# Side work of a Fourier-mixing and attention kernel moved to other steps, and two PSUM tags exchanged

## The chip, the core and the metric

The kernel runs on one core of a Trainium2 chip. The time is device microseconds (us) of one execution; three executions of the kernel before gave 740.35, 734.36 and 738.96, so the median is 738.96 us. Each core has a matrix engine (TensorE, PE in the profile, with PEld for the loading of weights), a vector engine (VectorE, DVE), a scalar engine (ScalarE, ACT), GpSimd (POOL) and SyncE (SP), which here only issues transfers. Every engine works through its own list of instructions in the order in which the program wrote them; engines wait for each other through semaphores.

## What is computed

The output is two results side by side. The first, A, is an attention with 32 heads of 18 columns over 2048 rows in four segments, with a memory that is carried from segment to segment. The second, B, filters x in the Fourier domain:

```
X = rfft2(x)             # x: 2048 x 576
X = X * (w_r + 1j * w_i) # 2048 x 289
y = irfft2(X, s=(2048, 576))
```

The change touches B's two transforms, the splitting of A's weights, and two small mask tiles of A.

## The kernel before

The order of the whole program is written out by hand: the scheduler leaves it as it stands, so each engine's list follows the order in which the Python code emits instructions. Four stages follow each other on the matrix engine.

**Forward transform (`forward`, L108 to L196).** The 2048 rows are 16 x 128, and unit u of 16 is one block of 128 rows. In step u of a loop over 20 steps, `f1(u)` multiplies the unit by the column tables in 14 matmuls into one of three two-bank PSUM tiles (tag f1), and `c1(u-3)` multiplies an older unit by its 128-point tables in 12 matmuls into two one-bank tiles (tag c1, two buffers). Float32 accuracy is kept by splitting every operand into a high and a low part, each rounded for the matmul. So around them run, in this order in a step: ACT's `ev0(u-1)`, which copies f1's result as X0, and `evz(u-4)`, which copies c1's result out as Z and so frees its banks; the first half of `prep(u+2)` (DVE sums and differences eo, L125; ACT's rounded copy eh, L127); DVE's `ev1(u-1)` (X1, the low part, L149); a call of the pace, below; the second half of `prep` (DVE el, L131 and L132); the matmuls of f1; a load of the next input or, from step 12, a step of `first` (loads and splits of A's first x); the matmuls of c1; a load of cfw; and from step 2 one step of `load_w`, which loads one tile of A's wqk and splits the tile that was loaded two steps before (`wsplit`: ACT copy L403, DVE subtraction L405; the last of five row blocks takes two DVE instructions of 64 partitions, L405 and L406). wqk has ten tiles, five row blocks by two column halves of 576.

**The pace.** The radix-4 butterflies and twiddles between the two transforms (`bf` L206, `tws`, `stage1`, `middle`, `last`) are generators of 266 steps in all, mostly one DVE instruction each, which work on Z in SBUF. `Pace.take(f)` runs f of them at the place where it is called. `projections` shares out what the forward loop left, less ten, evenly over its units.

**Projections (`projections`, from L533).** Four groups of 13 units: nine `qk_unit` (14 matmuls of 512 columns, then DVE and ACT work that splits the result in three, of which L478 is the DVE subtraction, L482 and L485 ACT copies and L484 a matmul that the next unit waits behind) and four `v_unit` (ACT copies L509 into tile vt, two buffers, which is stored to vD). In the last group a hook opens the pools of the inverse transform at unit 9 and from unit 11 calls `ysplit`, which splits a finished Z block into the high and low parts Y0 (ACT, L280) and Y1 (L281). `ysplit` runs the pace on until its group of four blocks has finished.

**Inverse transform (`inverse`, L283 to L341).** In step u, `i2(u,(0,1))` and `i2(u,(2,))` multiply Y(u) by tables civ in 12 and 6 matmuls into two PSUM tiles; ACT (L326, L333) and DVE (L328, L334) copy them out as T0 and T1 and free the two banks; `i3(u-2)` multiplies T by the tables itab in 14 matmuls into two more banks; `out` combines and stores. Two tags, i2 and i3, have two buffers each: the tag that is asked for first takes banks 3 and 4, the other 5 and 6. Beside it runs `prologue`, which starts A's attention with `s1`; its mask tiles tri and idb are made by `masks` (L582), and PE's first use of them is L645.

**Attention** follows, with 133 steps from 360 us on. The change does not touch it.

Of the kernel before, what the change touches and what calls it, by code (L numbers as in the profile page):

```python
# [5 lines left out]
F32=mybir.dt.float32; F32R=mybir.dt.float32r  # L6
# [96 lines left out]
class FFT:  # L103
# [4 lines left out]
    def forward(s,xp,cp,pp,wl,xs,consts):  # L108

        nc,io=s.nc,s.io; v=nc.vector  # L110
        xin={}; cw={}; C={}; eh={}; el={}; F={}; X={}
        def load(u):
            xin[u]=xp.tile([128,2,3,128],F32,name="xin",bufs=3)
            nc.sync.dma_start(xin[u],io["xb"][u])
        def loadc(u):
            a,b=BORD[u]
            cw[u]=cp.tile([128,2,384],F32R,name="cfw",bufs=4)
            nc.gpsimd.dma_start(cw[u],io["cfw"][4*a+b].rearrange("p (h m) -> p h m",h=2))
        def prep(u,halves=False):

            x=xin.pop(u)
            eo=xp.tile([128,2,3,128],F32,name="eo",bufs=2)
            h=xp.tile([128,2,3,128],F32R,name="eh",bufs=3)
            for r,op in enumerate((OP.add,OP.subtract)):
                v.tensor_tensor(eo[:,r],x[:,0],x[:,1],op=op)  # L125
                if halves: nc.scalar.copy(h[:,r],eo[:,r])
            if not halves: nc.scalar.copy(h,eo)  # L127
            yield
            l=xp.tile([128,2,2,128],F32R,name="el",bufs=3)
            for w in (slice(0,1),slice(1,2)) if halves else (slice(0,2),):  # L130
                v.tensor_tensor(l[:,w],eo[:,w,:2],h[:,w,:2].bitcast(F32),op=OP.subtract)  # L131
                v.tensor_tensor(h[64:97,w,2],eo[64:97,w,2],h[64:97,w,2].bitcast(F32),op=OP.subtract)  # L132
            eh[u],el[u]=h,l
            yield
        def f1(u):
            p=pp.tile([128,2,512],F32,name="f1",tag="f1")
            h,l=eh.pop(u),el.pop(u)
            for r in range(2):
                L=[(h[:,r,0],tab[:,0,r,0]),(h[:,r,1],tab[:,0,r,1]),(h[:,r,0],tab[:,1,r,0]),(h[:,r,1],tab[:,1,r,1]),
                   (l[:,r,0],tab[:,0,r,0]),(l[:,r,1],tab[:,0,r,1]),(h[:99,r,2],tab2[:99,r])]  # L140
                for n,(x,t) in enumerate(L):
                    nc.tensor.matmul(p[:,r,:FP],x,t,start=n==0,stop=n==6)  # L142
            F[u]=p
        def ev0(u):
            x=xp.tile([128,2,FP],F32R,name="X0",bufs=3); X[u]=[x]
            nc.scalar.copy(x,F[u][:,:,:FP])
        def ev1(u):
            x=xp.tile([128,2,FP],F32R,name="X1",bufs=3)
            v.tensor_tensor(x,F.pop(u)[:,:,:FP],X[u][0].bitcast(F32),op=OP.subtract)  # L149
            X[u].append(x)  # L150
        def evz(u):
            a,b=BORD[u]
            for r,p in enumerate(C.pop(u)): nc.scalar.copy(s.Z[:,b,a,r],p[:,:FP])
        def c1(u):
            a,b=BORD[u]; x=X.pop(u); cc=cw.pop(u)
            for r in range(2):
                p=pp.tile([128,512],F32,name="c1",tag="c1")
                n=0
                for (i,hl) in ((0,0),(0,1),(1,0)):
                    for q in range(2):  # L160
                        k=(0 if q==0 else 2) if r==0 else (1 if q==0 else 0)
                        nc.tensor.matmul(p[:,:FP],cc[:,hl,k*128:(k+1)*128],x[i][:,q],start=n==0,stop=n==5)
                        n+=1
                C.setdefault(u,[]).append(p)
        load(0)
        tab=cp.tile([128,2,2,2,FP],F32R,name="ftab",bufs=1)
        tab2=cp.tile([128,2,FP],F32R,name="ftab2",bufs=1)
        nc.gpsimd.dma_start(tab[:,0],io["ftab"][:,:4*FP].rearrange("p (r c f) -> p r c f",r=2,c=2))
        late=consts()
        nc.gpsimd.dma_start(tab[:,1],io["ftab"][:,4*FP:].rearrange("p (r c f) -> p r c f",r=2,c=2))  # L170
        nc.gpsimd.dma_start(tab2,io["ftab2"].rearrange("p (r f) -> p r f",r=2))
        load(1); load(2); late()
        for u in range(2): loadc(u)
        p=[prep(u,True) for u in range(2)]
        for i in range(2):
            for x in p: next(x)
        load(3)
        s.pace=Pace(61+165+40)
        for u in range(20):
            p=prep(u+2) if u+2<16 else iter(())  # L180
            if 0<u<17: ev0(u-1)
            if 3<u: evz(u-4)
            if u%4==3 and u>6: s.pace.add(s.stage1((u-7)//4))
            next(p,None)
            if 0<u<17: ev1(u-1)
            if u<14: s.pace.take(1)
            next(p,None)
            if u<16: f1(u)
            if u+4<16: load(u+4)
            elif u<18: next(xs,None)  # L190
            if 2<u<19: c1(u-3)
            if 0<u<15: loadc(u+1)
            if 1<u: next(wl,None)
            if u>13: s.pace.take(2)
        for _ in wl: pass
        for _ in xs: pass  # L196
    def bf(s,x,y,inv):
# [85 lines left out]
    def inverse(s,yl,pp):  # L283

        nc,io=s.nc,s.io; tab,tab2=s.itab,s.itab2; v=nc.vector
        T={}; po={}; Yt=s.Yt
        def i2(u,cs):
            Y=Yt[u]; cc=s.civ[u]
            p=pp.tile([128,len(cs),256],F32,name="i2",tag="i3" if u==1 else "i2")
            for k,c in enumerate(cs):  # L290
                n=0
                for (i,hl) in ((0,0),(0,1),(1,0)):
                    for q in range(2):
                        o=128 if q==0 else 0
                        m=128 if c<2 else 99
                        nc.tensor.matmul(p[:m,k],Y[i][:,q,c*128:c*128+m],cc[:,hl,o:o+256],start=n==0,stop=n==5)  # L296
                        n+=1
            return p
# [21 lines left out]
        for u in range(18):  # L320
            if u>15: flush()
            if u<16:
                h=yl.tile([128,3,256],F32R,name="T0",bufs=3); l=yl.tile([128,2,256],F32R,name="T1",bufs=3)
                T[u]=(h,l)
                p=i2(u,(0,1))
                nc.scalar.copy(h[:,:2],p)  # L326
                if u+2<16: s.ysplit(u+2)
                v.tensor_tensor(l,p,h[:,:2].bitcast(F32),op=OP.subtract)  # L328
                yield
                flush()  # L330
                p=i2(u,(2,))
                Yt.pop(u); s.civ.pop(u)
                nc.scalar.copy(h[:99,2],p[:99,0])  # L333
                v.tensor_tensor(h[64:97,2],p[64:97,0],h[64:97,2].bitcast(F32),op=OP.subtract)  # L334
                if u+4<16: s.load_civ(u+4)
                yield
            if u>1:
                yield from i3(u-2)
                out(u-2)
                s.pace.take(1)  # L340
# [44 lines left out]
class ATT:  # L385
# [21 lines left out]
    def load_w(s,nm,n,wp,st,w,tag,bufs):  # L407
        nc,io=s.nc,s.io
        s.wh[nm]=wp.tile([128,5,n],F32R,name=nm+"h"); s.wl[nm]=wp.tile([128,5,n],F32R,name=nm+"l")
        J=[(t,o) for t in range(5) for o in range(0,n,w)]; q=[]  # L410
        for i in range(len(J)+bufs-1):
            if i<len(J):
                t,o=J[i]
                x=st.tile([128,512 if tag=="xl" else w],F32,name="raw",tag=tag,bufs=bufs)[:,:w]
                nc.sync.dma_start(x,io[nm][:,t*n+o:t*n+o+w])
                q.append((t,o,x))
            if i>=bufs-1:
                t,o,x=q.pop(0)
                s.wsplit(nm,x,t,o,w)
            yield  # L420
# [451 lines left out]
    def prologue(s):  # L872

        nc,io=s.nc,s.io
        yield
        s.load_v(0)
        q=s.stack_dmas(1,0)+s.stack_dmas(1,1)+s.stack_dmas(2,0)+s.stack_dmas(2,1)+[lambda: s.load_v(1)]+s.stack_dmas(3,1)
        for i in range(2): yield
        s.masks()
        i=0  # L880
        for t in range(10):
            for _ in s.s1(t):
                for _ in range(1+(i%24==0)):
                    if q: q.pop(0)()
                i+=1
                yield
            if 2<=t<6: nc.gpsimd.dma_start(s.Ks[t-2][108:110].rearrange("p h c -> p (h c)"),io["neg1"])
            if t in (3,7): m=s.mpath(t//4); next(m)
            if t in (4,8): next(m); next(m,None)
        assert not q  # L890
# [147 lines left out]
def emit(nc,tc,io):  # L1038
    def pool(es,name,bufs=1,**kw):
        return es.enter_context(tc.tile_pool(name=name,bufs=bufs,reuse_waits="tile",**kw))  # L1040
    with ExitStack() as L0:
# [8 lines left out]
        F=FFT(nc,tc,io,zp); F.tp=A.ftp=ftp  # L1050
        with tc.manual_schedule():
# [5 lines left out]
            with ExitStack() as es:  # L1057
# [3 lines left out]
                def hook(g,i):  # L1061
                    if g==3 and i==9:
# [2 lines left out]
                        F.yp=pool(Ri,"yp",2); F.Yt={}; ci=pool(Ri,"ci")  # L1065
                        tc.swap_default_side()
                        F.inv_setup(ci)
                    if g==3 and i>10: F.ysplit(i-11,nc.vector)
                    if g==3 and i==0: q0.extend(A.stacks0(x0))
                    if g==3 and i>0: q0.pop(0)()  # L1070
                q0=[]
# [38 lines left out]
```

## Time and profile before

The profiled execution took 736.84 us; its instructions span 735.1 us, so 1.7 us lie around them. It lies 2.1 us below the median of the three executions.

| stage | on PE, us from the start |
|---|---|
| forward transform | 9.2 to 76.0 |
| projections | 76.0 to 284.3 |
| inverse transform, with the attention's prologue | 284.5 to about 360 |
| attention, output projections | to the end at 735.1 |

Over the span PE is busy for 691.1 us, DVE for 553.4, ACT for 457.9, POOL for 204.2. A row of the timeline gives the start in us, the duration in us of the merged group, engine, line, operation, out<-in with shapes, the count, and in brackets the idle time before it with what ended it. Matmuls overlap: the start of the next row, not the end of a row, tells when PE was free. Times of "waits" are us in total, number of times, and the longest.

### The profile page before, as it was taken

Reading aid. Unit: us, or ns where it says so; the run is one execution under the profiler, and the core shown is the slowest. Engines: PE = TensorE matmul, PEld = TensorE weight load, DVE = VectorE, ACT = ScalarE, POOL = GpSimd, SP = SyncE. Lnnn points to the kernel's source line nnn. Section 1 sums busy time; section 2 is a strip of 40 time slices with the busy share of each in tenths; the row PEclk is TensorE's granted clock in tenths of the full one; section 3 lists DMA queues with packets and bytes.
Section 4 is the critical chain, followed back from the end, with each engine's and each line's share of the span. In section 5 each row is a group of like instructions: output and inputs, shape, how many; then the busy total and the mean of one; then the engine's idle time right before and its main releaser. Section 6 shows DMA issues by size and latency. Waiting matters only on the chain.

```text
span 735.1 us, 14249 instructions
## 1 busy us (share of the span) xinstructions
PE 691.1 (94%) x4879; PEld 496.6 (68%) x4879; DVE 553.4 (75%) x1285; ACT 457.9 (62%) x1012; POOL 204.2 (28%) x405
## 2 busy tenths in 40 slices
PE   4998999999999999999999999999999899998897
PEld 4988779879779788899744444443665345653396
DVE  6999879899799788787688878876567575668333
ACT  3666796585585664444487777776566566568521
POOL 2111000100200112565065335462334832325100
PEclk9999999999999999999999999999999899999999
DMA  9884435655373468899547656777456565431231
GB/s 337 264 267 148 144 116 180 197 173 160 133 236 113 169 206 277 213 219 219 179 99 185 168 149 162 179 177 145 117 142 161 142 156 131 108 115 41 70 123 64
DMA packets 83243, 121.04 MB, mean 165 GB/s; under 512 B 11352, under 2 KB 50630, under 8 KB 83036
## 3 DMA queue, kind: packets, MB, share of 16 engines
q1 hardware_dynamic: 76580, 104.11, 49.9%
q0 software_dynamic: 6592, 16.03, 8.0%
q8 instruction: 38, 0.62, 0.3%
q14 instruction: 33, 0.27, 0.1%
HBM read 81.78 MB, written 38.24 MB: 163 GB/s over the span
## 4 chain that ended last, share of the span: by engine, by line
PE 70%; DMA 13%; DVE 7%; ACT 5%; issue 3%; POOL 1%; SPq 1%; ACTq 0%; DVEq 0%; POOLq 0%
PE pj L459 14%; PE pv L709 8%; PE po L829 7%; PE pjv L459 7%; PE s L636 4%; PE i L307 4%; PE i L296 3%; PE s L644 3%; PE s L679 3%; DMA x<-qkD 2%; DMA Ks<-qkD 2%; DMA Qs<-qkD 2%; PE pn L778 2%; PE po L858 2%; PE s L683 2%
## 5 line engine op out<-in xcount | busy, mean ns | idle before, releaser
L640 DVE CUSTOM_DVE_ANT_0 junk<-s,mask 128x512 bf16<-128x512 f32 (+1 forms) x256 | 141.2, 551 | 62.6 <-PE s L636 59.0
L646 DVE TENSOR_REDUCE mx<-s 128x4 f32<-128x512 f32 x128 | 87.9, 687 | 12.0 <-PE s L645 9.2
L692 POOL TENSOR_SCALAR_AFFINE_SELECT P<-P 128x512 f32<-128x512 f32 x116 | 70.0, 634 | 73.9 <-ACT P L680 66.0
L709 PE MATMUL pv<-P,vs 128*32 128x512 f32 (+3 forms) x1024 | 89.3, 445 | 0.3 <-DVE P L694 0.3
L680 ACT ACTIVATE P<-s 128x512 f32<-128x512 f32 x128 | 76.3, 596 | 17.4 <-PE s L679 15.0
L689 ACT ACTIVATE P<-s 128x256 f32<-128x256 f32 x128 | 49.1, 384 | 50.9 <-PE s L688 50.9
L685 ACT ACTIVATE P<-s 128x512 f32<-128x512 f32 x128 | 76.0, 594 | 0.3 <-PE s L684 0.3
L459 PE MATMUL pj<-x,wqkh 128*128 128x512 f32 x162 | 56.5, 409 | 0.0
L206 DVE TENSOR_TENSOR Z<-t,t 128x290 f32<-128x290 f32 (+1 forms) x96 | 48.4, 553 | 0.1
L206 DVE TENSOR_TENSOR t<-Z 128x580 f32<-128x580 f32 x64 | 46.0, 754 | 0.0
L506 POOL MEMSET vt<- 128x32 f32 x16 | 2.3, 161 | 153.8 <-PE pm L516 128.7
L636 PE MATMUL s<-Ks,Qs 108*128 108x512 bf16 (+1 forms) x128 | 42.2, 330 | 0.1
L142 PE MATMUL f<-ftab,eh 128*128 128x290 f32 (+1 forms) x160 | 31.4, 315 | 10.1 <-DMA ftab<-ftab 10.1
L296 PE MATMUL i<-civ,Y 128*128 128x256 f32 (+1 forms) x288 | 38.5, 285 | 1.5 <-POOL Y L281 0.9
L296 PEld LDWEIGHTS i<-civ,Y 128*128 128x128 f32 (+1 forms) x288 | 35.9, 181 | 2.3 <-POOL Y L281 1.3
L709 PEld LDWEIGHTS pv<-P,vs 128*32 128x32 f32 x1024 | 22.4, 109 | 21.9 <-issue 14.6
L645 PE MATMUL s<-tri,idb 128*128 128x256 bf16 x128 | 35.2, 275 | 1.3 <-ACT idb L585 1.3
L307 PE MATMUL i<-itab,T 128*128 128x290 f32 (+1 forms) x224 | 36.0, 309 | 0.0
L459 PE MATMUL pj<-xh,wqkl 128*128 128x512 f32 x90 | 35.5, 395 | 0.0
L459 PE MATMUL pj<-x,wqkl 128*128 128x512 f32 x90 | 35.5, 395 | 0.0
L459 PE MATMUL pj<-xh,wqkh 128*128 128x512 f32 x90 | 35.5, 395 | 0.0
L459 PEld LDWEIGHTS pj<-x,wqkh 128*128 128x128 f32 x162 | 30.4, 188 | 7.2 <-issue 0.6
(211 smaller groups left out, 1830.5 us busy)
## 6 DMA issues: line engine op xcount, KB each, us to landing
qkD<-sp SPq DMA_DIRECT2D x36, 384.0 KB
Ks<-qkD SPq DMA_DIRECT2D x72, 144.0 KB
x<-qkD SPq DMA_DIRECT2D x60, 144.0 KB
Qs<-qkD SPq DMA_DIRECT2D x60, 144.0 KB
xin<-xb SPq DMA_DIRECT2D x16, 384.0 KB
cfw<-cfw POOLq DMA_DIRECT2D x16, 384.0 KB, 4.9
civ<-civ POOLq DMA_DIRECT2D x16, 384.0 KB, 7.6
vs<-vD SPq DMA_DIRECT2D x16, 330.0 KB
```

What stands on the lines that cost most here:

```text
L206: v.tensor_tensor(o,a,b,op=op)
L296: nc.tensor.matmul(p[:m,k],Y[i][:,q,c*128:c*128+m],cc[:,hl,o:o+256],start=n==0,stop=n==5)
L307: nc.tensor.matmul(p,x,t,start=n==0,stop=n==6)
L459: s.nc.tensor.matmul(out,a,b,start=i==0,stop=i==len(L)-1)
L636: nc.tensor.matmul(out,Q[:108,h,128*i:128*i+128],K[:108,h,:128*(i+1)],start=True,stop=True)
L640: nc.vector.tensor_tensor_reduce(out=junk[:,:w],in0=src,in1=s.mask[:,512-w:],scale=1.0,scalar=-3.0e38, op0=OP.add,op1=OP.max,accum_out=s.m ...
L646: nc.vector.tensor_reduce(out=s.mx[k][:,hh],in_=pa.rearrange("p (b c) -> p b c",c=128),axis=mybir.AxisListType.X,op=OP.max)
L680: nc.scalar.activation(P[0][:,hh],p0,AF.Exp,scale=SC)
L685: nc.scalar.activation(P[1][:,hh],p1,AF.Exp,scale=SC)
L692: if k<29: nc.gpsimd.affine_select(out=x,in_=x,pattern=pat+[[1,128]],compare_op=OP.is_ge,fill=0.0,base=0,channel_multiplier=-1)
L709: nc.tensor.matmul(s.pvt[32*hh:32*hh+32,128*j:],vt[:,j,19*h:19*h+32],mv[0][:,hh,mv[1]],start=j==0,stop=j==2,skip_group_check=True)
L829: nc.tensor.matmul(ps,a[t][:r,c],b[:r,t,w],start=i==0,stop=i==14)
```

## The change

It does five things, and no instruction's shape changes.

1. In `forward`, steps 9 to 13 no longer call `load_w`; those calls come in steps 14 to 18. So tiles 5 to 9 of wqk are split five steps later, and tiles 7 to 9 are also loaded later: on SP's queue they now stand behind the last inputs and between the loads of A's first x. `load_w` goes over the column halves in its outer loop, so that the five tiles split early are the first half of the columns.
2. The pace's step at step 7 goes, and from step 14 it takes one step in place of two, then three in steps 18 and 19: 16 steps in the loop in place of 19.
3. `c1(14)` writes into an f1 tile in place of two c1 tiles.
4. In `inverse`, the tag i3 is used for the matmuls of u=0 in place of u=1. So u=0 takes banks 3 and 4 and u=1 banks 5 and 6 as before, but from then on `i2` uses banks 5 and 6, and `i3` banks 3 and 4.
5. Y(0), Y(1) and Y(2) are split in the last three units of the projections with DVE subtractions (before: Y(0) and Y(1), one unit later); Y(3) is split at the end of step 0 of the inverse with POOL subtractions, Y(4) in step 2. `masks` is emitted at the start of `prologue`'s work, one of its steps ahead of the first `s1`.

In each engine's list this comes to the following. PE: the same list, but for the 12 matmuls of `c1(14)` and the banks. ACT: the copies of the splits stand elsewhere; Y(0)'s copies now stand ahead of L482 of the last `qk_unit`, tri and idb behind the copies of u=2 and not behind those of u=3. POOL: two subtractions fewer. DVE: two subtractions more, and 32 steps of the pace in place of 27 between the last L478 of the projections and the first L328 of the inverse.

```diff
         def c1(u):
             a,b=BORD[u]; x=X.pop(u); cc=cw.pop(u)
+            if u==14: P=pp.tile([128,2,512],F32,name="f1",tag="f1")
             for r in range(2):
-                p=pp.tile([128,512],F32,name="c1",tag="c1")
+                p=pp.tile([128,512],F32,name="c1",tag="c1") if u!=14 else P[:,r]
...
-            if u<14: s.pace.take(1)
+            if 7<u<14: s.pace.take(1)
...
-            if 1<u: next(wl,None)
-            if u>13: s.pace.take(2)
+            if 1<u<9 or u>13: next(wl,None)
+            if u>13: s.pace.take(1 if u<18 else 3)
...
-            p=pp.tile([128,len(cs),256],F32,name="i2",tag="i3" if u==1 else "i2")
+            p=pp.tile([128,len(cs),256],F32,name="i2",tag="i3" if u==0 else "i2")
...
-                if u+2<16: s.ysplit(u+2)
+                if 1<u<14: s.ysplit(u+2)
...
                 v.tensor_tensor(h[64:97,2],p[64:97,0],h[64:97,2].bitcast(F32),op=OP.subtract)
+                if u==0: s.ysplit(3)
                 if u+4<16: s.load_civ(u+4)
...
-        J=[(t,o) for t in range(5) for o in range(0,n,w)]; q=[]
+        J=[(t,o) for o in range(0,n,w) for t in range(5)]; q=[]
...
         yield
+        s.masks()
         s.load_v(0)
...
         for i in range(2): yield
-        s.masks()
...
-                    if g==3 and i>10: F.ysplit(i-11,nc.vector)
+                    if g==3 and i>9: F.ysplit(i-10,nc.vector)
```

## The prediction

> **What bounds the kernel now.** I read the whole span first, then busy time by stage, then who waited for whom on PE, then the timelines of the two stages that the change touches.
>
> ```profile
> span 735.1 us, 14249 instructions
> 36.00:61.00 25.00, 23.28 (x163) 21.92 (x162) 24.60 (x43) 15.31 (x30) 3.17 (x6) 1.00 0.80 243
> 160.00:180.00 20.00, 20.00 (x148) 18.95 (x147) 19.60 (x36) 12.17 (x25) 0.17 (x2) 1.00 0.58 182
> 180.00:280.00 100.00, 99.46 (x556) 84.02 (x556) 84.10 (x158) 65.68 (x127) 10.88 (x40) 1.00 0.52 174
> 302.00:360.00 58.00, 57.90 (x452) 54.72 (x451) 44.97 (x110) 25.42 (x62) 27.01 (x39) 1.00 0.85 208
> PE c L162 <- ACT Z L153: 4.4, 8, 1.2
> PE s L645 <- ACT idb L585: 1.3, 1, 1.3
> ```
>
> The columns of a stretch are its length, then busy us of PE, PEld, DVE, ACT, POOL, then clock, DMA share, GB/s. In the projections (160 to 280) and the inverse (302 to 360) PE is the bound, at 99% and more, so time taken from other engines there is worth nothing. In 36 to 61, the second half of the forward transform, DVE is full (24.60 of 25) and PE is not. Of PE's waits, 4.4 us are c1's for the copies of Z, all in the forward transform, and 1.3 us are for idb at the start of the inverse. These stages can give something, and only these.
>
> ```profile
> 32.83 0.70 PE L142 MATMUL f<-ftab,eh 128*128 128x290 f32 x4
> 36.35 0.70 PE L142 MATMUL f<-ftab,eh 128*128 128x290 f32 x4
> ...
> 56.56 0.70 PE L142 MATMUL f<-ftab,eh 128*128 128x290 f32 x4
> 60.67 0.69 PE L142 MATMUL f<-ftab,eh 128*128 128x290 f32 x4
> 65.66 0.70 PE L142 MATMUL f<-ftab,eh 128*128 128x290 f32 x4
> 70.11 3.48 PE L162 MATMUL c<-X,cfw 128*128 128x290 f32 x24 [0.77 <-ACT Z L153]
> 74.32 1.88 PE L162 MATMUL c<-X,cfw 128*128 128x290 f32 x12 [0.73 <-ACT Z L153]
> 76.04 0.63 PE L459 MATMUL pj<-x,wqkh 128*128 128x512 f32 x2
> 31.10 1.02 DVE L125 TENSOR_TENSOR eo<-xin 128x384 f32<-128x384 f32 x2
> 34.93 1.02 DVE L125 TENSOR_TENSOR eo<-xin 128x384 f32<-128x384 f32 x2
> 43.17 1.02 DVE L125 TENSOR_TENSOR eo<-xin 128x384 f32<-128x384 f32 x2
> 46.62 0.76 DVE L405 TENSOR_TENSOR wqkl<-raw,wqkh 128x576 fp32r<-128x576 f32 x1
> 47.30 1.02 DVE L125 TENSOR_TENSOR eo<-xin 128x384 f32<-128x384 f32 x2
> 58.99 0.75 DVE L405 TENSOR_TENSOR wqkl<-raw,wqkh 64x576 fp32r<-64x576 f32 x1
> 45.02 0.67 ACT L403 CAST wqkh<-raw 128x576 fp32r<-128x576 f32 x1
> 46.13 0.70 ACT L153 COPY Z<-c 128x290 f32<-128x290 f32 x2
> ```
>
> The rows of L142 are f1(7), (8), (13), (14), (15). A step is 3.52 us while PE sets it (32.83 to 36.35), and 4.11 us in steps 9 to 13 (56.56 to 60.67). One DVE step is 4.13 us (43.17 to 47.30), of which the split of a weight tile is 0.68 (46.62 to 47.30), or 1.5 where it is two instructions of 64 partitions (0.75 each, 58.99). Without the split it would be 3.45, just under PE's 3.52.
>
> **The change, part by part.** (1) Forward, steps 9 to 13. The split goes: DVE 4.13 to 3.45, ACT's copy goes as well, and PE's 3.52 takes over. But step 8 now holds both a butterfly step and the two-instruction split. DVE's L125 of steps 6 and 7 lies 3.83 apart (31.10, 34.93); with no butterfly in step 7, step 8 starts at 34.93 + 3.83 = 38.76 and lasts 4.13 + 0.82 = 4.95, so the L125 of step 9 comes at 43.71. From such a row to the end of the Z copy that frees c1's bank are 3.3 us before (43.17, to 46.13 plus half of 0.70), 0.6 of it the weight copy of 45.02, which is gone in step 9. Hence c1 of step 10 starts at 43.71 + 2.7 + 0.1 = 46.5. With every step at 3.52, f1(10) would start at 36.35 + 7.04 = 43.4 and its c1 1.8 later (3.52 less 1.74, half of the 24 matmuls of 70.11), at 45.2: PE comes 1.3 late, once, and DVE then keeps ahead. f1(14) starts at 36.35 + 6 x 3.52 + 1.3 = 58.8 in place of 60.67.
>
> (2) Forward, steps 14 to 18. The step from f1(14) to f1(15) took 4.99, as its DVE work held a 1.5 split; now 3.52, so f1(15) starts at 62.3, 3.4 early. The 0.77 wait of c1(13) stays: its bank comes free only behind the X0 copy that waits for c1(12). c1(15) now needs the copy of unit 13, not 14, which stood behind A's x splits: its 0.73 goes. The projections start at 76.04 - 3.4 - 0.73 = 71.9: **4.1 us earlier**. The moved splits (0.67 ACT, 0.68 to 1.5 DVE each) lie beside the matmuls: after step 13 DVE has no more prep, and X1, a split of x, a split of wqk and a butterfly, each like the rows of 0.7 to 0.8, make some 3 us a step. The first unit needs only the first column half, split by step 8; the second is needed by unit 4, 14 us later. The loads of tiles 7 to 9 follow A's x on SP's queue and have two steps to land; the x loads behind them are used at 71.9 + 2 us or later. If that cover fails the price is the lateness of one load, 0 to 2 us; the trace shows no such wait, and I take 0. The bank for c1(14) held f1(13), read out long before: 0.
>
> (3) Three butterfly steps pass from the loop to the projections, about 2 us on a DVE that is idle for 15.9 us in 180 to 280: 0.
>
> (4) The inverse's start.
>
> ```profile
> 284.53 4.53 PE L296 MATMUL i<-civ,Y 128*128 128x256 f32 x36 [0.22 <-ACT vt L509]
> ...
> 293.10 2.04 PE L307 MATMUL i<-itab,T 128*128 128x290 f32 x14
> 294.97 2.30 PE L296 MATMUL i<-civ,Y 128*128 128x256 f32 x18
> 297.11 0.39 PE L644 MATMUL s<-x 108*128 108x384 bf16 x2
> 272.14 2.91 DVE L206 TENSOR_TENSOR Z<-t,t 128x580 f32<-128x580 f32 x6
> 274.97 2.77 DVE L206 TENSOR_TENSOR t<-Z 128x580 f32<-128x580 f32 x4
> 277.67 1.08 DVE L281 TENSOR_TENSOR Y<-Z,Y 128x512 fp32r<-128x512 f32 x2
> ...
> 285.19 2.54 DVE L206 TENSOR_TENSOR Z<-t,t 128x580 f32<-128x580 f32 x5
> 288.61 0.69 DVE L328 TENSOR_TENSOR T<-i,T 128x512 fp32r<-128x512 f32 x1 [0.88 <-ACT T L326]
> 289.78 0.43 DVE L334 TENSOR_TENSOR T<-i,T 33x256 fp32r<-33x256 f32 x1 [0.49 <-ACT T L333]
> 271.59 0.59 ACT L482 CAST sp<-pj 128x512 bf16<-128x512 f32 x1
> 289.56 1.83 POOL L281 TENSOR_TENSOR Y<-Z,Y 128x512 fp32r<-128x512 f32 x2 [1.83 <-ACT Y L280]
> ```
>
> PE does i2(0) and i2(1) in one run, 36 matmuls. i2(2) is 18 matmuls, 2.14 us where nothing holds it (294.97 to 297.11), but PE reached i3(0) only at 293.10, as Y(2) was still being split. Now Y(2) is ready before. What is late next is DVE. Its list from 272.14 runs without a gap to 287.7 (285.19 plus 2.54) and then starts L328. The list now holds five more butterfly steps and Y(2)'s subtractions: four of t, 2.70 (274.97 to 277.67), one of Z, 0.37 (2.91 less 2.54), and the 1.08 of 277.67, together 4.15 us. It ends at 291.9, and L328(0), L334(0), L328(1) follow in 0.69 + 0.43 + 0.69, less overlaps of 0.1, to 293.6. This matters because of the exchanged tags: i2(2) now goes into the bank that i2(1) filled, and must wait for L328(1), where before it went into i2(0)'s. So i2(2) starts at 293.6 and i3(0) at 293.6 + 2.14 = 295.7, not 293.10: **2.6 us lost**. Five butterfly steps fewer in the inverse save nothing, as PE is full there.
>
> (5) Masks. tri and idb are copied behind u=2, before PE comes to L645: the 1.30 us goes. Their two copies then delay only E(0), for which nothing waits.
>
> (6) ACT's copies of Y(0) now stand before L482 of the last qk unit and wait for DVE's first Z of 272.14: L482 moves from 271.59 to some 2.5 us later, and all of PE's v matmuls stand behind the L484 that needs it. PE reached L484 about then, so this costs from 0 to the 0.7 of one copy; I take 0.2, an estimate. The copies of vt behind L482 come later too, and with them one store; the copies that wait for its slot come long before DVE's 293.6, which covers this.
>
> (7) POOL: its two subtractions of Y(2) go; the load of civ for u=4 now stands behind Y(3)'s, about as before behind Y(2)'s. 0.
>
> Sum: -4.1 + 2.6 - 1.3 + 0.2 = **-2.6 us**. Against the profiled execution (span 735.1, time 736.84) that is a span of 732.5 and a time of 734.2; the median of the executions lies 2.1 above it, so I forecast 736.4.
>
> **A rule weighed.** Y(3)'s subtractions on POOL (1.83 us for the pair) now fall beside DVE's last butterfly steps.
>
> ```profile
> 192.70 0.82 DVE L206 TENSOR_TENSOR t<-Z 128x580 f32<-128x580 f32 x1
> 192.86 0.72 POOL L532 TENSOR_TENSOR zst<-mm,zst 126x7 f32<-126x7 f32 x1
> ```
>
> Where the two engines met, DVE's instruction took 0.82 (0.76 without), and POOL's 0.72. By the rows POOL gives way, which costs the sum 0.1. [...]
>
> **The rivals.**
> - POOL holds DVE up in the last steps: both subtractions, 1.83 us, go into DVE's list and so into i2(2)'s start: -2.6 + 1.8 = -0.8, 738.2. For it: POOL's start falls among four back-to-back steps. Against: the pair of rows above.
> - DVE's list is not the wait: i2(2) runs at once behind the 36 matmuls, at 288.9, and i3(0) at 291.0, a gain of 2.1 in place of the loss of 2.6: -7.3, 731.7. For it: Y(2) is ready, and 4.7 us of PE time hang on this. Against: DVE's list, which has no gap from 272.14 on.
> - The forward step does not fall, because the ring of X0, Z and c1 and not DVE's load sets it: only 0.73 and the 1.5 of step 14 are gained: -2.2 + 1.5 = -0.7, 738.3. Against: step 7 ran at 3.52 with the split and without the butterfly.
> - Slower: ACT's L482 behind Y(0). If DVE reaches the butterflies of 272.14 late by x, L482, L484 and all of PE behind it are late by x. It decides from x = 2.6. At x = 4, twice the 2 us of the deferred steps, the time is 738.96 + 1.4 = 740.4. For it: DVE was at 19.60 of 20 in 160 to 180. Against: 15.9 us idle in 180 to 280.
>
> **How the numbers follow.** Forecast 0.55; POOL ahead 0.13; no DVE wait 0.14; forward unchanged 0.10; slower 0.08. The forecast's own range is 734.5 to 738, from the bounds in parts 2 and 6 and half of the once-late 1.3 us. The range for 8 in 10 reaches up to the slower rival's near side and down to the case without DVE's wait: 731.5 to 739.5. One per cent, about what a measurement of this kernel can tell from no change (its three executions span 6 us), is 7.4 us: below 731.6 lies half of the case without DVE's wait and a rest for terms that I have too small, 0.13; above 746.3 nothing that I can work out, 0.05; between, 0.82.
>
> **What would show each step.** Steps of 3.5 us from f1(10) to f1(15), one wait of about 1 us in c1 of steps 9 and 10, projections from about 72 us; no wait of c1(15). A wait of PE's L296 for DVE's L328 of about 4.5 us, the longest of that stage, with DVE busy without a gap up to it; no wait for idb. POOL's subtractions of Y(3) longer than 1.83 us. The forecast is wrong if i2(2) starts before DVE's butterflies end, or if the projections start later than 73 or lose their 99%.

## The result and the profile after

The changed kernel takes 740.41 us (median of 20 executions, 737.53 to 743.52); the kernel before, in 20 executions (the three of the first section among them), 736.8. The ratio is 1.004, with a 95% interval of 1.0026 to 1.0054: slower by 1.9 to 4.0 us. The forecast was 2.6 us faster. The profiled execution took 738.24 (span 736.5). Times here are medians of all executions of a run; a ratio is worked out from the single executions, without the few in which the chip was in a slower state (one of the twelve behind the 734.04 of the run with Y(2) and Y(3) on DVE), and so is not just the quotient of two medians.

A caution for all places below: PE's first waits, for the column tables, take between 8.7 and 10.1 us in all in eight of the runs (10.1 before, 9.8 after). So places of two runs agree only to 1 or 1.5 us; lengths and waits are better compared.

The waits on PE and the busy time by stretch, with the columns of the prediction. L-numbers after the change are one or two higher than before: L480, L484, L486 are the subtraction, the second copy and the last matmul of a qk unit; L297 is i2, L329 and L335 the subtractions on T.

```profile
PE i L297 <- DVE T L329: 5.1, 1, 5.1
PE pj L486 <- ACT sp L484: 4.1, 5, 1.8
PE c L163 <- ACT Z L153: 1.4, 2, 0.8
PE i L297 <- ACT vt L511: 1.3, 1, 1.3
PE pm L518 <- ACT pk L497: 0.6, 1, 0.6
36.00:61.00 25.00, 24.25 (x174) 23.32 (x174) 24.25 (x43) 15.38 (x32) 3.70 (x7) 1.00 0.72 220
76.00:160.00 84.00, 80.28 (x430) 65.77 (x429) 73.69 (x141) 63.61 (x125) 2.75 (x18) 1.00 0.48 161
280.00:302.00 22.00, 15.66 (x110) 15.20 (x109) 16.97 (x29) 6.87 (x18) 6.20 (x12) 0.84 0.56 170
```

The forward transform gained what was meant: c1 waits 1.4 us in place of 4.4, and the wait for idb is gone. But two waits grew or are new: 4.1 us for the qk units' second copies, and 5.1 us for DVE at the inverse. The stretch 280 to 302 shows something that no part of the prediction had: a granted clock of 0.84. The timeline of PE, at the four places that matter:

```profile
58.80 0.70 PE L142 MATMUL f<-ftab,eh 128*128 128x290 f32 x4
62.32 0.69 PE L142 MATMUL f<-ftab,eh 128*128 128x290 f32 x4
66.76 1.87 PE L163 MATMUL c<-X,cfw 128*128 128x290 f32 x12 [0.77 <-ACT Z L153]
71.69 0.63 PE L461 MATMUL pj<-x,wqkh 128*128 128x512 f32 x2
81.73 0.38 PE L486 MATMUL pj<-sp,nid 128*128 128x512 bf16 x1 [1.71 <-ACT sp L484]
96.04 0.38 PE L486 MATMUL pj<-sp,nid 128*128 128x512 bf16 x1 [0.21 <-ACT sp L484]
105.99 0.38 PE L486 MATMUL pj<-sp,nid 128*128 128x512 bf16 x1 [1.80 <-ACT sp L484]
273.60 0.38 PE L486 MATMUL pj<-sp,nid 128*128 128x512 bf16 x1 [0.22 <-ACT sp L484]
284.52 4.51 PE L297 MATMUL i<-civ,Y 128*128 128x256 f32 x36 [1.25 <-ACT vt L511]
294.11 4.16 PE L297 MATMUL i<-civ,Y 128*128 128x256 f32 x18 [5.08 <-DVE T L329]
298.10 2.04 PE L308 MATMUL i<-itab,T 128*128 128x290 f32 x14
303.42 0.39 PE L638 MATMUL s<-x 108*128 108x512 bf16 x1
```

f1(14), f1(15) and the projections start at 58.80, 62.32 and 71.69; the forecast had 58.8, 62.3 and 71.9. Then the three waits of 81.73, 96.04 and 105.99 take back 3.7 us (before, 0.27 + 0.96). The first two of the next rows are of the kernel before, the others of the changed kernel; they show the stretch, what DVE did ahead of the first wait, and the busy times around the waits:

```profile
76.00:160.00 84.00, 82.63 (x439) 67.80 (x438) 71.90 (x137) 63.27 (x126) 3.04 (x18) 1.00 0.52 169
80.25 0.69 DVE L478 TENSOR_TENSOR pj<-pj,sp 128x512 f32<-128x512 f32 x1
...
73.96 2.78 DVE L207 TENSOR_TENSOR t<-Z 128x580 f32<-128x580 f32 x4
76.66 2.54 DVE L207 TENSOR_TENSOR Z<-t,t 128x580 f32<-128x580 f32 x5
79.86 0.69 DVE L480 TENSOR_TENSOR pj<-pj,sp 128x512 f32<-128x512 f32 x1
...
80.00:90.00 10.00, 8.29 (x37) 6.39 (x36) 9.12 (x20) 9.14 (x21) 0.00 (x0) 1.00 0.64 196
100.00:110.00 10.00, 8.20 (x46) 6.77 (x45) 5.93 (x13) 9.53 (x20) 0.00 (x0) 1.00 0.31 107
```

The projections start 4.35 us earlier, but the first subtraction of a qk unit only 0.4 (79.86 against 80.25): nine butterfly steps, 5.2 us in a row, stand in front of it. Near 106 it is ACT that is busy (9.53 of 10), not DVE (5.93). At the inverse, i2(2) starts at 294.11, and its 18 matmuls take 4.16 us, where 18 such matmuls took 2.30 before. What DVE and POOL did just ahead of it:

```profile
287.03 1.20 DVE L207 TENSOR_TENSOR Z<-t,t 128x290 f32<-128x290 f32 x3
288.14 4.14 DVE L207 TENSOR_TENSOR t<-Z 128x580 f32<-128x580 f32 x4
292.20 0.68 DVE L329 TENSOR_TENSOR T<-i,T 128x512 fp32r<-128x512 f32 x1
288.52 2.47 POOL L282 TENSOR_TENSOR Y<-Z,Y 128x512 fp32r<-128x512 f32 x2 [2.12 <-ACT Y L281]
```

Four steps of t took 4.14 us where four took 2.77 before: 1.37 more, just while POOL subtracted for Y(3), itself 2.47 in place of 1.83. And the clock, from the windows of 0.4 us around its two edges:

```profile
291.00:291.40 0.40, 0.00 (x0) 0.00 (x0) 0.40 (x1) 0.00 (x0) 0.40 (x1) 0.81 0.87 261
291.40:291.80 0.40, 0.00 (x0) 0.00 (x0) 0.40 (x2) 0.00 (x0) 0.40 (x2) 0.50 1.09 347
...
297.40:297.80 0.40, 0.40 (x4) 0.40 (x3) 0.11 (x1) 0.40 (x2) 0.00 (x0) 0.50 0.00 0
297.80:298.20 0.40, 0.40 (x4) 0.40 (x3) 0.40 (x1) 0.38 (x1) 0.00 (x0) 0.65 0.00 0
```

0.81 in a window is full clock for 0.25 of its 0.4 us and half clock behind, so the clock fell at 291.25; by 0.65 it came back at 298.08. It was halved for 6.83 us, two times the 3.41 of a run below. i2(2) lies wholly inside. From these rows i3(0) starts 5.00 us later than before (298.10 against 293.10). The masks give 1.46 of it back: the score matmul of 512 columns (L638, before L636) behind the first masked one started at 299.88 before, and starts at 303.42 here, 3.54 later. This profiled execution regains 2.1 us of that in the attention, which I didn't follow; the medians differ by 3.6.

### The profile page after: what moved, and what is told of

It is laid out like the page before. It is cut to its first block, busy times and chain, and to the rows that moved or that the text cites. A ratio compares the mean times of both kernels' runs of the same rounds, so it can differ in the third digit from the quotient of the medians.

```text
span 736.5 us, 14243 instructions
## 1 busy us (share of the span) xinstructions
PE 690.8 (94%) x4879; PEld 497.6 (68%) x4879; DVE 555.6 (75%) x1287; ACT 457.6 (62%) x1012; POOL 202.2 (27%) x403
## 4 chain that ended last, share of the span: by engine, by line
PE 51%; DVE 7%; DMA 5%; ACT 2%; issue 2%; POOL 1%; SPq 0%; DVEq 0%; ACTq 0%; POOLq 0%
PE pv L711 9%; PE po L831 7%; PE s L638 5%; PE i L297 4%; PE i L308 4%; PE pj L461 3%; PE s L646 3%; PE s L681 3%; PE pn L780 2%; PE s L685 2%; PE po L860 2%; DMA Qs<-qkD 2%; DVE t L207 2%; PE s L647 1%; DVE junk L642 1%
## 5 line engine op out<-in xcount | busy, mean ns | idle before, releaser
L694 POOL TENSOR_SCALAR_AFFINE_SELECT P<-P 128x512 f32<-128x512 f32 x116 | 70.0, 634 | 71.9 <-ACT P L682 64.1
L297 PE MATMUL i<-civ,Y 128*128 128x256 f32 (+1 forms) x288 | 39.7, 293 | 6.3 <-DVE T L329 5.1
L638 PE MATMUL s<-Ks,Qs 108*128 108x512 bf16 (+1 forms) x128 | 42.2, 330 | 0.1
L297 PEld LDWEIGHTS i<-civ,Y 128*128 128x128 f32 (+1 forms) x288 | 37.4, 189 | 6.8 <-DVE T L329 5.3
```

What stands on the lines that cost most here:

```text
L638: nc.tensor.matmul(out,Q[:108,h,128*i:128*i+128],K[:108,h,:128*(i+1)],start=True,stop=True)
L694: if k<29: nc.gpsimd.affine_select(out=x,in_=x,pattern=pat+[[1,128]],compare_op=OP.is_ge,fill=0.0,base=0,channel_multiplier=-1)
```

## The experiments

Theory A, from these rows: four things turned a gain into a loss. The first qk units come too early for DVE and ACT (2.5 us more of waits); DVE's list ahead of the inverse is longer, as predicted; POOL lengthens it by 1.4; and PE, standing still behind it, gets a half clock that costs 1.9. The rivals are with each run.

**The two halves.** First the forward hunks alone, then the inverse hunks alone, each on the kernel before.

```diff
-            if u<14: s.pace.take(1)
+            if 7<u<14: s.pace.take(1)
-            if 1<u: next(wl,None)
-            if u>13: s.pace.take(2)
+            if 1<u<9 or u>13: next(wl,None)
+            if u>13: s.pace.take(1 if u<18 else 3)
... (and c1(14), load_w)
```

> The forward part of the change alone (items 1 to 3), on the inverse of the kernel before. Theory A (DVE comes late to the first units of the projections, and this takes back more than half of the forward gain): projections start at about 71.7 as in the changed kernel, against 76.0 before; PE again waits about 1.7 us at the third matmul of the first qk unit and about 1.8 us near 106, against 1.2 us in all before; the v projections end about 1.4 us early. PE's first i2 starts between 283.1 and 284.5, as the copies of vt wait for stores; no wait of 5 us at the inverse and a full clock there. Time 0 to 1.4 us below the kernel before, 735.4 to 736.8. Theory B (the forward part gains its 4.1 us and all of the loss is in the inverse): 732.7.

Measured: ratio to before 0.9977 (0.9951 to 1.0003), or 1.7 us faster, with the waits of the first units at 3.7 us and no half clock at the inverse (1.00 in 280 to 302). The 4.1 of theory B (a ratio of 0.994) lies outside the interval, no change just inside it: less than the whole gain arrives, and how much does is not known more closely.

```diff
-            p=pp.tile([128,len(cs),256],F32,name="i2",tag="i3" if u==1 else "i2")
+            p=pp.tile([128,len(cs),256],F32,name="i2",tag="i3" if u==0 else "i2")
-                    if g==3 and i>10: F.ysplit(i-11,nc.vector)
+                    if g==3 and i>9: F.ysplit(i-10,nc.vector)
... (and the other splits, masks)
```

> The inverse part of the change alone (items 4 and 5), on the forward transform of the kernel before. Theory A (DVE's list is longer by five butterfly steps and Y(2), is lengthened once more by 1.4 us where POOL works on Y(3), and the wait of 5 us brings a half clock that costs 2 us): DVE's list ends 0.9 us later than in the changed kernel, i2(2) starts at about 295, with 0.5 of the clock for some 4 to 6 us, and takes about 4 us in place of 2.2; the masks give back 1.3 to 1.5. Sum 2.6 + 0.9 + 1.4 + 2.0 - 1.4 = +5.5; time 741 to 742.5. Theory B (the inverse part costs what the prediction said, 2.6 - 1.3 + 0.2): +1.5, 738.3.

Measured: 1.0034 (1.001 to 1.0058), 2.5 us slower. The interval, 0.7 to 4.3 us, leaves out theory A's 5.5 and takes in theory B's 1.5, so the time does not choose; the rows show the wait for DVE and the half clock of theory A, and say why it was less:

```profile
288.75 2.10 DVE L206 TENSOR_TENSOR t<-Z 128x580 f32<-128x580 f32 x3
289.42 3.12 POOL L281 TENSOR_TENSOR Y<-Z,Y 128x512 fp32r<-128x512 f32 x2 [2.12 <-ACT Y L280]
292.69 3.67 PE L296 MATMUL i<-civ,Y 128*128 128x256 f32 x18 [3.26 <-DVE T L328]
```

Here DVE's steps kept their 0.7 us each and POOL's pair took 3.12 (1.83 before): this time POOL gave way. The half clock came all the same (0.50 in 292.2 to 295.4). By their ratios the halves make +0.8 us together and the whole +2.9; with intervals of 2 us to either side for each half, that is no contradiction.

**The wait and the clock.** In the next run the pace leaves as many butterfly steps to the inverse as before the change.

```diff
+                if g==3 and i>9: w*=.78
                 advance()
                 pace.take(w*.4)
```

> The changed kernel with a lower pace in the last three v units, so that 11 butterfly steps (as before) in place of 6 are left for the inverse. Theory A: DVE's list ends near 288, PE's wait for DVE's subtraction on T(1) falls from 5.1 to 1 us or less, and with it the half clock goes: i2(2) starts near 289.7 in place of 294.1 (4.4 us) and takes 2.2 in place of 4.2 (2.0 us): 740.4 - 6.4 = 734.0. Theory B (the half clock has another cause than the wait): 740.4 - 4.4 = 736.0. Theory C (another thing is late next at this place, POOL's Y(3) or a load of civ): 737 to 738, with its name in PE's waits.

Measured: 0.9971 (0.9945 to 0.9997), 735.45. The wait fell to 1.83 us, not under 1, and the clock was halved all the same (0.50 in 291.4 to 294.2):

```profile
290.15 3.44 PE L297 MATMUL i<-civ,Y 128*128 128x256 f32 x18 [1.83 <-DVE T L329]
289.41 0.69 DVE L329 TENSOR_TENSOR T<-i,T 128x512 fp32r<-128x512 f32 x1 [0.55 <-DMA vD<-vt]
291.00:291.40 0.40, 0.40 (x5) 0.40 (x4) 0.00 (x0) 0.00 (x0) 0.00 (x0) 0.66 1.01 315
294.20:294.60 0.40, 0.40 (x4) 0.40 (x4) 0.38 (x1) 0.32 (x2) 0.40 (x1) 0.58 0.00 0
```

Late next, for 0.55 of the 1.83 us, was a store of a v tile (theory C had other names for it); that T1 of u=1 takes over the memory of that tile is inferred from this wait. The clock was halved from 291.13 to 294.54, 3.41 us (a later expectation calls a stretch of this length a window): so here it came behind 1.83 us of standing still. Whether standing still is the cause was tried by filling the changed kernel's wait with 36 repeated matmuls.

```diff
-                for (i,hl) in ((0,0),(0,1),(1,0)):
+                for (i,hl) in ((0,0),(0,1),(1,0))*(7 if u==1 and c==2 else 1):
+                    n%=6
```

> The changed kernel, in which PE does the last six matmuls of i2(1) seven times over (36 repeated matmuls, 4.3 us at full clock, same result), just where it waits for DVE. The wait for DVE's subtraction stays where it ends, 294.1. Theory A (PE's clock falls because PE stands still for 5 us): the clock stays at 1.00 and i2(2) takes 2.1 to 2.3 us in place of 4.16: 740.4 - 2.0 = 738.4, with more work on PE. Theory B (the clock falls for another reason): it falls again, no change, 740.4 or more.

Measured: 1.0004 (0.9983 to 1.0026), 737.58; by the ratios about 2.7 us less than the changed kernel, with more work on PE.

```profile
288.51 2.78 DVE L207 TENSOR_TENSOR t<-Z 128x580 f32<-128x580 f32 x4
289.33 3.67 POOL L282 TENSOR_TENSOR Y<-Z,Y 128x512 fp32r<-128x512 f32 x2 [2.11 <-ACT Y L281]
280.00:302.00 22.00, 21.29 (x170) 20.59 (x169) 17.95 (x34) 8.49 (x22) 8.91 (x14) 1.00 0.68 207
```

The clock is 1.00 in the whole stretch, where it was 0.84 in the changed kernel. Theory A holds: with the wait of 5.08 us filled, no half clock comes. Not all of the 2.7 us is the clock's, though. DVE's and POOL's lists are those of the changed kernel, but this time POOL gave way (3.67) and DVE's four steps took 2.78, so that DVE's list ended 1.0 us earlier (291.20 against 292.20). Next, the lower pace together with the banks of the kernel before, so that i2(2) waits for T(0) alone.

```diff
-            p=pp.tile([128,len(cs),256],F32,name="i2",tag="i3" if u==0 else "i2")
+            p=pp.tile([128,len(cs),256],F32,name="i2",tag="i3" if u==1 else "i2")
```

> The run with the lower pace in the last three v units, and with the banks of the kernel before: i2(1) in the i3 banks, so that i2(2) waits for the subtractions on T(0) and not on T(1). Theory A (what was late next there was the store of the last vt, which held the subtraction on T(1) to 289.41, and half a window of standing still is enough for the half clock): i2(2) starts at about 288.9, PE stands still under 1 us there, the clock stays at 1.00; 1.2 us of wait and 1.8 us of half clock go: 735.5 - 3.0 = 732.5. Theory B (the tag matters little, as i3(0) or i2(3) then waits for the same store): no gain or under 1 us, 734.5 to 735.5, with the wait at i3(0).

Measured: 0.9943 (0.9923 to 0.9964), 734.05.

```profile
284.60 6.66 PE L297 MATMUL i<-civ,Y 128*128 128x256 f32 x54 [1.06 <-ACT vt L511]
```

i2(0), i2(1) and i2(2) run as one group of 54 matmuls, and no half clock comes (1.00 in 280 to 302). With these two edits the rest of the change is a gain of 4 us.

**What held DVE?** DVE in place of POOL subtracts for Y(3) in the changed kernel.

```diff
-                if u==0: s.ysplit(3)
+                if u==0: s.ysplit(3,v)
```

> The changed kernel with the subtractions of Y(3) on DVE in place of POOL. Theory A (the butterfly steps that took 4.14 for four, and not 2.78, were held by POOL's subtractions): no such step is longer than 0.76 now, the subtraction on T(0) starts at 290.8 (1.4 earlier), and behind Y(3)'s 1.0 us that on T(1) starts at 293.0 to 293.4, as late as before within 0.4: 739.9 to 740.4. Theory B (they were long for a reason of DVE's own or of a memory): they stay long, the subtraction on T(1) starts at 294.4: 741.4.

Measured: 1.0041 (1.0023 to 1.0058), the time of the changed kernel, as theory A has it.

```profile
289.34 2.77 DVE L207 TENSOR_TENSOR t<-Z 128x580 f32<-128x580 f32 x4
```

The four steps of t took 2.77 again. So it was POOL's work that made them long. By what way POOL holds DVE, no run shows. No time is gained, as DVE now does the subtractions itself.

**The first units of the projections.** Four butterfly steps fewer at the end of the forward loop:

```diff
-            if u>13: s.pace.take(1 if u<18 else 3)
+            if u>13: s.pace.take(1)
```

> The changed kernel with one butterfly step instead of three in each of the last two steps of the forward loop; four butterfly steps (about 2.2 us of DVE) pass into the projections, so that DVE is free earlier for the subtraction of the first qk unit. Theory A (the butterflies that stand in front hold up the first units): PE's first wait for the second sp copy, 1.71 at 81.7, falls to 0.5 or less; the one near 106, where ACT's queue of twiddle copies is in front, stays within 1 us of what it was; the list of the inverse gains nothing. 740.4 - 1.3 = 739.1. Theory B (the projections simply start too early for the weights and x tiles that are split beside them): the wait stays, 740.4, or returns in the next unit.

Measured: 1.0038 (1.001 to 1.0066), 740.61. The first wait went, and 1.18, 0.62 and 1.12 came at 87, 103 and 109, 2.9 in place of 3.7, with 0.94 for a copy of pk at 119. The little that PE won became a longer wait for DVE at the inverse (6.6 us). That is what theory B has, but four steps may have been too few; the dealing below tells more. The same edit in the version with the lower pace and the banks of before:

> The three together: lower pace in the last three v units, banks of the kernel before, one butterfly step in the last two steps of the forward loop; everything else as changed. If the terms add: 732.5 - 1.3 = 731.2, about 0.8% below the kernel before and faster than both. If what the forward part wins is taken back by DVE or by the stores of v, as half of it was in the changed kernel: as the run without the last edit, 732.5.

Measured: 0.995 (0.9922 to 0.9978), 733.59: the terms don't add. The edit in the forward part, with only the masks of the inverse part:

```diff
         yield
+        s.masks()
         s.load_v(0)
...
         for i in range(2): yield
-        s.masks()
```

> The forward part with one butterfly step in the last two steps, and of the inverse part the masks alone (splits and banks as in the kernel before). The forward part alone gave 735.0; the masks take away PE's wait of 1.3 us for idb, and the last edit of the loop about 1.3: 732.4. If copying the masks earlier only moves ACT's work before the copies of T and E (rival), the wait at this place comes back under another name and the time is 733.7.

Measured: 0.9939 (0.9918 to 0.996), 732.52; the wait for idb is gone and 2.9 us remain at the first units. The diff of the masks alone, on the kernel before:

> The masks alone moved ahead, all else as in the kernel before. As the prediction's part 5 has it: PE's wait of 1.3 us for idb goes and nothing takes its place: 1.3 below the kernel before, ratio 0.998. Rival (the two copies, 0.5 us on ACT, hold up the copies of T that stand behind them): no change.

Measured: 0.9968 (0.9946 to 0.9991); the interval takes in the predicted 0.998. Now the dealing of the first nine units, on the kernel with the forward part and the masks:

```diff
-                w=tot/(36+16*2.4)*(1.0 if i<9 else 2.4)
+                w=tot/(36+16*2.4)*(1.0 if i<9 else 2.4)*(0.5 if g==0 and i<9 else 1.069)
```

> The kernel with the forward part, one butterfly step in the last steps and the masks ahead, in which the first nine units of the projections deal half as many butterfly steps (14 fewer), and all later units 6.9% more. Theory A (in 75 to 110 DVE and ACT are full, and the butterflies with their twiddle copies are what is too much): the 3.1 us that PE waits for the second sp copy fall to 1 or less, the projections end 2 us earlier: 732.5 - 2.1 = 730.4. Theory B (the splits of wv and x and the units' own copies are too much already): the waits stay within 0.5 us, 732.5. Theory C (later units, with 6.9% more, become late in turn): waits of the same kind after 120, 732 to 734.

Measured: 0.9983 (0.9965 to 1.0001), 735.81, slower than without the edit. On its own subject theory A was right: one wait of 0.64 up to 120 in place of 2.9 us, and the first i2 at 279.9 in place of 282.1. What ate it stands in the inverse:

```profile
284.03 5.73 DVE L207 TENSOR_TENSOR Z<-t,t 128x580 f32<-128x580 f32 x6
283.89 2.32 POOL L282 TENSOR_TENSOR Y<-Z,Y 128x512 fp32r<-128x512 f32 x2 [1.84 <-ACT Y L281]
286.75 1.94 POOL L282 TENSOR_TENSOR Y<-Z,Y 128x512 fp32r<-128x512 f32 x2
290.46 3.86 PE L297 MATMUL i<-civ,Y 128*128 128x256 f32 x18 [6.06 <-issue]
```

As PE came earlier, POOL's subtractions for Y(2) and Y(3) came earlier too, beside DVE's list. Six steps of Z, 2.91 before, took 5.73; PE stood still for 6.06 us and got the half clock (0.50 in 287.0 to 293.8). The same kernel with those subtractions on DVE:

```diff
-                if u+2<16: s.ysplit(u+2)
+                if u+2<16: s.ysplit(u+2,v if u<2 else None)
```

> The kernel with the forward part, the masks and half the butterfly steps in the first nine units (735.8), in which DVE and not POOL subtracts for Y(2) and Y(3). There DVE's last six butterfly steps took 5.73 in place of 2.91 while POOL worked on Y(2) and Y(3). Theory A (POOL's subtractions, come beside DVE's list because PE was early, held it): the six steps take 2.9 again, and behind Y(2)'s 1.0 us i2(2) starts near 289.0 in place of 290.5: 734.4. Theory B (the steps are slow for another reason): they stay slow, and the added 2 us of DVE make it 736 to 738.

Measured: 0.9969 (0.9943 to 0.9996), 734.04, as theory A has it; the six steps took 2.91. The same dealing in the version with the lower pace and the banks of before:

> The same dealing in the first nine units, in the kernel with the whole change, the lower pace in the last three v units and the banks of the kernel before. Theory A: 3 of the 4.2 us of waits go; PE comes that much earlier to the copies of vt, for which it waits 1.1 already and whose stores may not come earlier, so that 1.5 to 3 us reach the end: 731 to 732.5, against 734.05 without. Theory B: as without, 734.

Measured: 0.9941 (0.9919 to 0.9963), 731.95. The first units wait 0.7 us in all, but one wait of 2.9 us is new:

```profile
273.08 0.38 PE L486 MATMUL pj<-sp,nid 128*128 128x512 bf16 x1 [2.91 <-ACT sp L484]
271.54 1.01 ACT L281 CAST Y<-Z 128x512 fp32r<-128x512 f32 x2 [4.39 <-DVE Z L207]
```

That is the prediction's slower rival: ACT's second copy of the last qk unit behind Y(0)'s copies, which wait for DVE. In the changed kernel PE came 3 us later to this place, and the wait was 0.22. Two runs at the end put that copy ahead of Y(0), the second with a shorter DVE list as well:

```diff
-                    if g==3 and i>9: F.ysplit(i-10,nc.vector)
...
-                if g==3 and i>9: w*=0.78
+                if g==3 and i>9: w*=0.5      # second run only
                 advance()
+                if g==3 and i>9: split(i)
...
-                s.pace.take(1)
+                s.pace.take(2 if u<8 else 1) # second run only
```

> The best run so far (732.0: whole change, lower pace in the last three v units, banks of the kernel before, half the steps in the first nine units), with the split of Y(0) put behind the last qk unit's second sp copy and no longer ahead of it. There PE waited 2.9 us at 273 for that copy, which stood behind Y(0)'s copies on ACT. Theory A (DVE's list, which ends at 287.6 whatever PE does, sets when i2(2) starts): the wait at 273 goes, PE comes 2.9 us earlier to the inverse and stands still there for as long, with a half clock on top: 732 to 734. Theory B (the wait at 273 reaches the end): 729.

Measured: 0.9998 (0.9979 to 1.0017), 736.14, worse than without: theory A, and more, as POOL held DVE once more (six steps of Z in 4.27, against 2.91) and PE stood still for 4.65 us, with a clock of 0.50 behind it.

> The same with 17 in place of 10 butterfly steps left for the inverse, dealt two at a time in its first steps. Theory A (DVE's list is what the run before waits for): the list ends some 3.5 us earlier, at 284, i2(2) follows i2(1) at once at full clock, and what the store of vt leaves of the 2.9 us reaches the end: 729.5 to 730.5. Theory B (the seven steps come back in the inverse, where DVE was at 15.4 of 18 us): PE waits for DVE after 300, 732 or more.

Measured: 0.9903 (0.9879 to 0.9927), 730.11 (six executions), the fastest: 1% below the kernel before.

```profile
PE i L297 <- DVE T L329: 0.9, 1, 0.9
279.52 4.43 PE L297 MATMUL i<-civ,Y 128*128 128x256 f32 x36
284.84 2.41 PE L297 MATMUL i<-civ,Y 128*128 128x256 f32 x18 [0.89 <-DVE T L329]
```

With 17 steps left, DVE's list ends about when PE comes: 0.89 us of wait is left at i2(2), as theory A has it, and no half clock comes at the inverse (1.00 in 280 to 298). The seven steps found room in the inverse, where the profile lists no wait of PE from there to 354 us.

## Why the prediction was wrong

| term | forecast, us | profiled execution, us |
|---|---|---|
| 1, 2: projections start earlier | -4.1 | -4.35, of which 0.3 is the wait for the tables |
| 3: waits of the first units | 0 | +2.5 (3.72 against 1.23) |
| 6: second copy behind Y(0) | +0.2 | +0.22 |
| 4: DVE's list and the tags | +2.6 | length as predicted, start not: see below |
| POOL holds DVE | 0 | +1.37 |
| half clock in i2(2) | not seen | +1.9 (4.16 less 2.30) |
| 5: masks | -1.3 | -1.46 |

With 2.6 for the list, the right column sums to +2.8; 3.54 was measured behind the masks. PE's places do not simply add, as i2(2) starts when DVE's list ends. Along that list the sum comes out. The forecast puts i2(2) at 293.6 - 4.1 = 289.5 and i3(0) at 291.6; measured are 294.11 and 298.10. Of the 4.6 us that i2(2) is late, 3.2 are the list's start (271.27, where the forecast implies 272.14 - 4.1 = 268.0) and 1.4 are POOL's; the half clock adds 1.9 to i3(0).

- **Parts 1 and 2, the forward steps:** the places of f1(14), f1(15) and the projections are right to 0.2, for f1(14) partly by luck: f1(8) came 0.4 earlier than taken (35.95 against 36.35), and PE was late by 1.7 up to f1(14) and not by 1.3, spread over several steps and not once. The cover of the moved splits failed in part: the last one, 72.39 to 73.94, lies behind the start of the projections.
- **The step that failed first is part 3:** "Three butterfly steps pass from the loop to the projections, about 2 us on a DVE that is idle for 15.9 us in 180 to 280: 0". The cover was read from the wrong stretch. The prediction's rows of stretches leave out 76 to 160, where PE was busy for 82.63 of 84 us before and for 80.28 after: the projections lost their 99%, one of its own signs of being wrong. The steps, the last of the five weight splits and a PE that comes 4 us early meet in 72 to 110, where waits for the same copy stood in the trace before; no run separates the three. Halving the butterflies there left one wait of 0.64 us, and 6.9% more of them later gave only one of 0.64 at 195, where the kernel before had 0.54.
- **Part 4, the list:** the mechanism, the waiting instruction (the forecast's L328(1), now L329(1)) and the list's length are as forecast: 20.9 us from its first Z, of which 1.37 were POOL's, against 19.8. **The sum failed with part 3:** to add -4.1 to +2.6 takes for granted that DVE's list starts 4.1 us earlier, as PE does. Its first Z came 0.87 earlier (271.27 against 272.14). Nor does it follow when PE's waits are gone: with half the steps in the first units the first i2 came 2.2 us earlier than without (279.88 against 282.06), the first Z 0.1 (270.98 against 271.08); the same number of steps lay ahead of it, dealt later.
- **The rule weighed.** I took the one pair of rows in which POOL gave way (0.72 us for L532, whose median is 0.20) as the rule. The runs show either engine held: DVE in the changed kernel (4.14 us for the steps of 2.77), POOL in the inverse part alone (3.12 for the pair of 1.83). The price of 0 in the sum was too low; whether the chance of 0.13 was, one outcome does not tell.
- **The half clock had no place in the sum.** The trace of before shows a low clock in the attention, 0.69 in 580 to 590, just behind a wait of PE of 1.51 us that ended at 579.68. With a wait of 4.5 us in the forecast, that was reason enough to put in a price for it.
- **Part 5:** right. **Part 6:** 0.22 for 0.2, by luck, as PE came late to this place. The slower rival didn't decide here; it did at 2.9 us in the run where PE came early. That its time, 740.4, is the one measured is chance as well.

What stays open: how often POOL holds DVE over many executions (one profile each was seen), how much standing still halves the clock, and the 2.1 us which the profiled execution regains in the attention.

## What to carry to other kernels

When a stage is made to end earlier, read the cover of every moved instruction in the stretch into which it moves, not in a later one: here DVE's idle 15.9 us lay 100 us behind the place of need. Where PE hands over to another engine's list, gains ahead of it are worth little until that list is shortened, and a wait there can cost more than its length: the waits of 1.83 to 6.58 us at the inverse had a clock of 0.50 behind them in seven profiles. So shorten the list first, and then gain time ahead of it.

## What the runs showed of the hardware

- **PE's clock was halved behind waits of less than 2 us.** The half clock lasted 3.41 us or twice that (291.13 to 294.54 with the lower pace, 291.25 to 298.08 after). With the lower pace, one wait of 1.83 us, which ended at 290.15, stood ahead of the fall at 291.13. In the masks' run it was three waits, 1.68 us together:

```profile
290.06 0.75 PE L296 MATMUL i<-civ,Y 128*128 128x256 f32 x4 [0.76 <-ACT Y L280]
291.45 0.38 PE L296 MATMUL i<-civ,Y 128*128 128x256 f32 x1 [0.65 <-POOL Y L281]
292.10 2.50 PE L296 MATMUL i<-civ,Y 128*128 128x256 f32 x13 [0.27 <-POOL Y L281]
292.60:293.00 0.40, 0.40 (x6) 0.40 (x5) 0.00 (x0) 0.00 (x0) 0.40 (x1) 0.90 0.67 178
```

  The fall is at 292.92. In the forward part alone 0.61 + 0.27 us at this place left the clock at 1.00. But the length of the waits does not decide alone: the changed kernel's waits of 1.71 and 1.80 us, which end at 81.73 and 105.99, are longer than the three, and yet the clock in 80 to 90 and 100 to 110 is 1.00 (rows above). What else counts, no run shows.
- **Which of DVE and POOL is held is not fixed by their lists.** Held DVE: 1.37 us in the changed kernel, 2.82 where two pairs of subtractions met the list (5.73 less 2.91). Held POOL: 3.12 in place of 1.83 in the inverse part alone, and 3.67 in the run with repeated matmuls, whose DVE and POOL lists are those of the changed kernel, both with DVE's steps unchanged.
